# Spreading VectorE's share of the softmax evenly, and running the third query block in halves, in a fused attention and gated-MLP block

## The chip, the cores and the metric

One core of a Trainium2 chip runs the whole program. The metric is the device time of one execution in microseconds; the time before is 909.33 us, the median of three runs (908.4, 909.33 and 910.13).

## The reference, cut to what matters

```python
# S = 2048 rows, D = 640, H = 32 heads of Dh = 20, F = 1728, bf16, one batch
def attention(x, wqkv, wo):
    q, k, v = split_heads(x @ wqkv)                          # each (H, S, Dh)
    p = softmax(einsum("hqd,hkd->hqk", q, k) * Dh ** -0.5)
    return merge_heads(p @ v) @ wo
def glu(x, w_gate, w_up, w_down):
    return ((x @ w_gate) * (x @ w_up)) @ w_down
h  = x + attention(layernorm(x), wqkv, wo)
h2 = h + glu(layernorm(h), w_gate, w_up, w_down)             # the output
```

The two layer norms have no scale and no offset.

## The kernel before

**Units.** The scores of one head for 512 keys-by-queries are the unit of work: a 128x512 tile in PSUM, made of 128 keys and 512 queries, or of two times 128 keys and 256 queries where a pass works on half a query block. There are 2048 such units (32 heads, 16 key tiles, 4 query blocks). Four heads share a group, because a head takes 32 of the 128 partitions (`SLOT`); there are 8 groups (`g` = 0 to 7).

**Segments.** The list `segs` gives the order: for each segment a pass (`PASS`: its query block, first column and width), a group and a range of key tiles. Query block 0 starts in chunks of four key tiles for groups 0 to 3, since keys and values are projected while attention already runs; the rest of block 0, and blocks 1 and 2, go group by group over all 16 key tiles (passes "0", "1", "2": "whole" segments of 64 units). Block 3 goes whole for groups 0 and 1 (`SPLIT_G` = 2, pass "3") and then in halves: pass "A" has its first 256 queries for groups 2 to 7, pass "B" the other 256 ("half" segments of 32 units). Below, A4 is group 4 of pass A.

**Two exponentials.** Most units get their exponential on ScalarE (`nc.scalar.activation`, line 676), three and two units at a time in alternating steps; a step `i` is one such activation, fed by TensorE's score products (line 668). Some units of a segment instead go to VectorE: `on_dve(s)` says how many. Such a unit's scores go to a bank of the ring `mi` (two PSUM banks that all projection and MLP sums use too); VectorE takes them out (line 688, tile `di`), and after every second unit a batch of three integer and bf16 passes follows (lines 571, 573, 576), whose results `dt` and `di` stand for the exponential together. Before the change `on_dve` counts in whole key tiles (four units): 12 of 64 units in a whole segment, and in half segments 8 of 32 for even groups and 4 of 32 for odd ones, none in the chunks; 336 in all. `due` says at which ScalarE unit each VectorE unit is to be issued; `EARLY` and `LEAD` are how far ahead of the segment's start the first is due and how far ahead of its end the last.

**Accumulation.** `emit_AV` multiplies exponentials with values (line 802) into one PSUM bank `acc`. A segment's last product closes it (`close`): VectorE copies the bank to `asb` (line 819), and only then can the next segment's products start. The normalization follows by small DMAs and GpSimd (`norm`), or through TensorE for the segments in `FAST` (`job_norm`).

**Jobs.** All other TensorE work is a queue of jobs, a few products at a time put between the steps by a planner with costs of its own (`fill_step`, `can_work`): projections (`job_proj`, `job_V`), and for each query block a tail (`add_tail`): output projection, layer norm, the gated product (`job_glu`: `u` and `hh`, line 1095) and the last product (`job_y`). A tail is queued once all segments of its rows are normalized: blocks 0, 1 and 2 as a whole with four row tiles, block 3's first half after pass A. The second half of block 3 has a tail of its own behind everything (`last_tail`).

**The head.** The layer norm of the first 512 rows comes first; then steps run while the queue makes four value jobs, and after them the projections of groups 1 to 3. The layer norm of rows 512 to 1023 gets its inverse root by a chain of Newton steps on VectorE (`rstd_steps`), the later ones on GpSimd (`rstd_wait`).

All engines work through their instructions in the order in which the program issues them.

Of the kernel before, what the change touches and what calls it, by code (L numbers as in the profile page):

```python
# [10 lines left out]
BF16 = mybir.dt.bfloat16  # L11
F32 = mybir.dt.float32
I32 = mybir.dt.int32
# [5 lines left out]
P = 128  # L19
# [19 lines left out]
FP = 7  # L39
FPW = 256  # L40
G1 = 4
SPLIT_G = 2
QA = 3 * QB
RES0 = 3
SM_SCALE = float(DH) ** -0.5
# [10 lines left out]
EXP_BIAS = KAPPA - 127.0 * math.log(2.0)  # L56
DB = 2
DW = DB * BANK
LEAD, EARLY = 18, 6
SWITCH = 100  # L60
ROUND = 216
S_NS = SWITCH + ROUND
# [2 lines left out]
EASE, HURRY = -400, -200  # L65
S_LAG = 270
AHEAD = 700
MINJOB = 800
AVLOW = 8
AVMIN = 216  # L70
SLACK = 100
# [5 lines left out]
def kernel(  # L77
# [114 lines left out]
            nc.vector.bn_stats(st[:, h, :], halves[h] if halves else src[:, h * HALF:(h + 1) * HALF])  # L192
        nc.vector.bn_aggr(mv[:, k, :], st[:])

    def rstd_steps(mv, n):
        mb = small.tile([P, n], BF16, name="mb")
        nc.vector.tensor_copy(mb[:], mv[:, :, 0])
        m32 = small.tile([P, n], F32, name="m32")
        nc.vector.tensor_copy(m32[:], mb[:])
        vb = small.tile([P, n], BF16, name="vb", tag="mvb")  # L200
        nc.vector.tensor_copy(vb[:], mv[:, :, 1])
        ve = small.tile([P, n], BF16, name="ve")
        nc.vector.tensor_scalar_add(ve[:], vb[:], EPS_B)
        v = small.tile([P, n], F32, name="v")
        nc.vector.tensor_copy(v[:], ve[:])
        yield
        y = small.tile([P, n], F32, name="y")
        iy = small.tile([P, n], I32, name="iy", tag="mb")
        nc.vector.tensor_scalar(iy[:], v[:].bitcast(I32), 1, None, ALU.arith_shift_right)
        nc.vector.tensor_scalar(y[:].bitcast(I32), iy[:], -1.0, float(0x5F3759DF), ALU.mult, ALU.add)  # L210
        t = small.tile([P, n], F32, name="nt")
        for k in range(3):
            nc.vector.tensor_tensor(t[:], y[:], y[:], ALU.mult)
            nc.vector.scalar_tensor_tensor(t[:], t[:], -0.5, v[:], ALU.mult, ALU.mult)
            nc.vector.scalar_tensor_tensor(y[:], t[:], 1.5, y[:], ALU.add, ALU.mult)
            if k == 0:
                yield
        den = small.tile([P, n], BF16, name="den")
        nc.vector.tensor_tensor(den[:], v[:], y[:], ALU.mult)
        r = small.tile([P, n], F32, name="rstd")  # L220
        nc.vector.reciprocal(r[:], den[:])
        yield (m32, r)

    def rstd_pool(mv, n):
        mvb = small.tile([P, n, 2], BF16, name="mvb", tag="mvb")
        nc.gpsimd.tensor_copy(mvb[:], mv[:])
# [10 lines left out]
    def rstd_wait(mv, n):  # L237
# [2 lines left out]
        while clk["dve"] < until and not forced["on"]:  # L240
            yield WAIT
        yield got

    def rstd_of(mv, n):
        for got in rstd_steps(mv, n):
            pass
        return got

    def ln_apply(dst, src, m32, r, k):
        nc.vector.tensor_scalar(dst, src, m32[:, k:k + 1], r[:, k:k + 1], ALU.subtract, ALU.mult)  # L250
# [120 lines left out]

    PASS = {"0": (0, 0, QB), "1": (1, 0, QB), "2": (2, 0, QB), "3": (3, 0, QB), "A": (3, 0, HW), "B": (3, HW, HW)}
    segs = []
    for ch in range(NB):
        for g in range(G1):
            kind = "copy" if ch == 0 else "last" if ch == NB - 1 else "add"
            segs.append(("0", g, ch * TPB, (ch + 1) * TPB, kind))
    segs += [("0", g, 0, NT, "only") for g in range(G1, NG)]  # L380
    segs += [(p, g, 0, NT, "only") for p in "12" for g in range(NG)]
    segs += [("3", g, 0, NT, "only") for g in range(SPLIT_G)]
    segs += [(p, g, 0, NT, "only") for p in "AB" for g in range(SPLIT_G, NG)]
    FINAL = len(segs) - 1
    FAST = {("2", NG - 1), ("A", NG - 1), ("B", NG - 2)}

    def on_dve(s):
        p, g, lo, hi, kind = segs[s]
        if kind != "only":
            return 0  # L390
        if PASS[p][2] == HW:
            return 2 - g % 2 if s != FINAL else 1
        return 3

    a_units, d_units, due, left = [], [], [], {}
    for s, (p, g, lo, hi, _) in enumerate(segs):
        n = BANK // PASS[p][2]
        groups = list(range(lo, hi, n))
        cut = len(groups) - on_dve(s)
        a0 = len(a_units)  # L400
        a_units += [(s, kt, j) for kt in groups[:cut] for j in range(HPG)]
        own = [(s, kt, j) for kt in groups[cut:] for j in range(HPG)]
        span = len(a_units) - a0
        due += [a0 - EARLY + (span - LEAD + EARLY) * (k + 0.5) / len(own) for k in range(len(own))]
        d_units += own
        left[s] = [n * (cut + 2 * on_dve(s))] * HPG

    LAST_B, LAST_T = NB - 1, [2, 3]
    first_b = [next(k for k, u in enumerate(us) if all(PASS[segs[v[0]][0]][0] == LAST_B for v in us[k:])) for us in (a_units, d_units)]
# [18 lines left out]
    def add(key, gen, front=False):  # L428
        (jobs.appendleft if front else jobs.append)((key, gen, None))
# [471 lines left out]
    def gen_ln(ch):  # L901
        ts = range(ch * TPB, (ch + 1) * TPB)
        while hold(("x", ch)):
            yield WAIT
        mv = small.tile([P, TPB, 2], F32, name="mv")
        for k in range(TPB):
            bn(mv, k, xs[ch][:, k, :])
            yield 930
        for got in (rstd_steps if ch == 1 else rstd_wait)(mv, TPB):
            yield WAIT if got == WAIT else 1100 if ch == 1 else 0  # L910
# [24 lines left out]
    def need_T(key, ch):  # L935
        needs[key] = T_keys(ch)
        return key

    for ch in range(NB):
        if ch:  # L940
            for t in range(ch * TPB, (ch + 1) * TPB):
                add(("T", t), T_of(t))
            if ch + 2 < NB:
                do(("x", ch + 2), lambda ch=ch: more_x(ch + 2))
            add(need_T(("k", 0, ch), ch), job_proj(1, 0, ch))
        for t in range(ch * TPB, (ch + 1) * TPB):
            add(need_T(("v", t, 0), ch), job_V(t, 0))
        for g in range(1, G1):
            if ch == 0:
                add(need_T(("q", 0, g), 0), job_proj(0, g, 0))  # L950
            add(need_T(("k", g, ch), ch), job_proj(1, g, ch))
    for g in range(G1, NG):
        add(need_T(("q", 0, g), 0), job_proj(0, g, 0))
        for ch in range(NB):
# [184 lines left out]
    def add_tail(b, ts):  # L1139
        if b == 0:  # L1140
            do(("open",), open_late)
        key = (b, ts[0])

        def loads():
            if b not in tail_st:
                tail_st[b] = new_st(rows_of(b))
                tail_st[b]["res"] = late["res"]
            load_tail(tail_st[b], ts)
            for fp in range(2):
                load_w(fp, tail_st[b])  # L1150
# [12 lines left out]
        add(("y",) + key, lazy(lambda st: job_y(st, ts)))  # L1163
# [74 lines left out]
    def normed(p, gs):  # L1238
        return all(("n", p, g) in done for g in gs)

    def add_tails():
        if seen["b"] < NB - 1 and normed(str(seen["b"]), range(NG)):
            add_tail(seen["b"], list(range(TPB)))
            seen["b"] += 1
        if not seen["a"] and normed("3", range(SPLIT_G)) and normed("A", range(SPLIT_G, NG)):
            add_tail(LAST_B, [0, 1])
            seen["a"] = True
# [17 lines left out]
    seen = {"b": 0, "a": False, "last": False}  # L1265
    i = 0
    while pos["a"] < len(a_units) or pos["d"] < len(d_units):
        now["i"] = i
# [14 lines left out]
    while acc["next"] < len(segs) or ("loadB",) not in done:  # L1283
        now["i"] = i
        clk["pe"] += 500
        clk["dve"] = max(clk["dve"], clk["pe"])
        act_end[i] = max(clk["pe"], *ring["free"]) + 3000
        work(i)
        emit_AV(i, 2, True)
        dve_fill(act_end[i], True)  # L1290
        run_events(i)
        add_tails()
        i += 1
# [99 lines left out]
```

## Time and profile before

| | |
|---|---|
| median of three runs | 909.33 us |
| the profiled execution's own time | 908.28 us |
| its span in the profile | 906.3 us |
| TensorE busy | 812.8 us (90%) |
| ScalarE busy | 807.9 us (89%) |
| VectorE busy | 712.7 us (79%) |
| GpSimd busy | 182.3 us (20%) |
| first and last exponential on ScalarE start | 17.3 and 846.2 us |
| ScalarE exponentials | 342 of 128x1536 and 343 of 128x1024 |
| VectorE units | 336 |

The profile is of one execution. Its times are microseconds from the span's start; a line of the timeline gives start, length, engine, source line, operation, output and input tile, the number of instructions merged, and in brackets the idle time before them and what ended it. TensorE's busy time is modelled from pipelined products and does not mean that the engine is at its peak.

### The profile page before, as it was taken

To read this page: it belongs to the slowest core of one execution; us is meant where nothing else is said; L and a number is where in the kernel's file an instruction comes from. 1 tells how busy PE (TensorE), PEld (TensorE's weight loads), DVE (VectorE), ACT (ScalarE), POOL (GpSimd) and SP (SyncE) were. 2 spreads that over 40 slices of the span, in tenths; PEclk is the share of its full clock that TensorE was granted. 3 is DMA by queue.
4 is the path that set the end of the run, shared out by engine and by line. 5 is a ranking of instruction groups with operands and counts; after the bars stand their busy time and mean duration, and the time that the engine had idled before them with its cause. 6 is when DMAs were issued, how large, how long until landed. Compare 5 with 4: busy or idle time off the path is not lost. (4 is left out here: it accounts for less than half of the span.)

```text
span 906.3 us, 27993 instructions
## 1 busy us (share of the span) xinstructions
PE 812.8 (90%) x12193; PEld 358.7 (40%) x12205; DVE 712.7 (79%) x1407; ACT 807.9 (89%) x721; POOL 182.3 (20%) x227
## 2 busy tenths in 40 slices
PE   6999999989999899998897988899988988998997
PEld 4343343322334233333243322344433444545775
DVE  7884449898888998987879978978898787789642
ACT  5899999999999999999999999999998888899331
POOL 3110025412213322212214210212041211214000
PEclk8999999999999999999999999999999999999999
DMA  6100001110080322101220121104401000031210
GB/s 197 30 3 1 3 16 27 36 29 14 14 286 16 111 72 73 36 21 30 64 58 3 53 65 45 33 21 114 120 14 44 9 9 22 17 98 51 72 44 18
DMA packets 67856, 45.08 MB, mean 50 GB/s; under 512 B 18504, under 2 KB 63404, under 8 KB 67728
## 3 DMA queue, kind: packets, MB, share of 16 engines
q1 hardware_dynamic: 67728, 43.23, 16.9%
q8 instruction: 97, 1.59, 0.7%
q14 instruction: 31, 0.25, 0.1%
HBM read 35.91 MB, written 7.30 MB: 48 GB/s over the span
## 5 line engine op out<-in xcount | busy, mean ns | idle before, releaser
L676 ACT ACTIVATE E<-sc 128x1536 bf16<-128x1536 f32 (+1 forms) x685 | 790.6, 1253 | 40.4 <-PE mi L668 22.5
L688 DVE TENSOR_SCALAR di<-mi 128x512 int16<-128x512 f32 x336 | 228.2, 683 | 37.8 <-PE mi L668 36.5
L668 PE MATMUL sc<-qa,kT 32*128 32x512 bf16 x1296 | 202.2, 383 | 45.1 <-ACT E L676 39.9
L802 PE MATMUL acc<-E,vx 128*32 128x512 bf16 (+1 forms) x2024 | 228.6, 354 | 6.1 <-DVE asb L819 3.1
L668 PEld LDWEIGHTS <-kT 32*128 32x128 bf16 x2432 | 81.0, 91 | 263.3 <-issue 254.4
L710 POOL TENSOR_TENSOR rr<-rr,powers 128x16 f32<-128x16 f32 (+1 forms) x34 | 90.5, 2661 | 324.4 <-DMA rr<-sums 324.4
L576 DVE TENSOR_TENSOR di<-di,dm 128x1024 bf16<-128x1024 bf16 x168 | 119.2, 709 | 3.9
L802 PEld LDWEIGHTS <-vx 128*32 128x32 bf16 x2840 | 70.3, 95 | 120.0 <-issue 106.7
L668 PE MATMUL mi<-qa,kT 32*128 32x512 bf16 x240 | 92.0, 383 | 0.9 <-DVE di L688 0.8
L293 PE MATMUL mi<-lnT,wp 128*32 128x512 bf16 x1240 | 80.6, 384 | 1.4 <-DVE lnT L265 0.7
L571 DVE TENSOR_SCALAR dm<-di 128x1024 int16<-128x1024 int16 x168 | 77.3, 460 | 2.8
L802 PE MATMUL acc<-dt,vx 128*32 128x512 bf16 (+1 forms) x408 | 74.5, 348 | 0.5 <-DVE dt L573 0.5
L573 DVE TENSOR_SCALAR dt<-di 128x1024 int16<-128x1024 int16 x168 | 74.7, 445 | 0.0
L802 PE MATMUL acc<-di,vx 128*32 128x512 bf16 (+1 forms) x408 | 72.6, 346 | 1.7 <-DVE di L576 1.4
L668 PE MATMUL sc<-qb,kT 32*128 32x256 bf16 (+1 forms) x728 | 65.4, 289 | 8.6 <-ACT E L676 7.7
L293 PE MATMUL mi<-wd,hh 128*32 128x320 bf16 x1391 | 63.9, 304 | 1.4 <-DVE di L688 1.0
L293 PEld LDWEIGHTS <-hh 128*32 128x32 bf16 (+1 forms) x1489 | 46.6, 97 | 21.8 <-issue 8.9
L293 PE MATMUL mi<-ln2T,wu 128*32 128x512 bf16 (+1 forms) x780 | 50.3, 370 | 4.4 <-DVE ln2T L265 1.6
L293 PE MATMUL mi<-ln2T,wg 128*32 128x512 bf16 (+1 forms) x780 | 48.7, 364 | 2.3 <-DVE u L265 1.3
L1095 DVE TENSOR_TENSOR hh<-mi,u 128x512 bf16<-128x512 f32 (+3 forms) x56 | 34.8, 621 | 15.8 <-PE mi L293 14.5
L265 DVE CAST u<-mi 128x512 bf16<-128x512 f32 (+3 forms) x56 | 34.7, 620 | 15.5 <-PE mi L293 15.0
L293 PEld LDWEIGHTS <-wp 128*32 128x32 bf16 x1240 | 31.9, 97 | 32.4 <-issue 10.4
(135 smaller groups left out, 683.1 us busy)
## 6 DMA issues: line engine op xcount, KB each, us to landing
bc<-scr SPq DMA_DIRECT2D x100, 64.0 KB
wu<-in_B_w_up_dram SPq DMA_DIRECT2D x20, 320.0 KB
wg<-in_B_w_gate_dram SPq DMA_DIRECT2D x20, 320.0 KB
qsp<-qa SPq DMA_DIRECT2D x8, 384.0 KB
xr<-in_A_x_dram SPq DMA_DIRECT2D x16, 160.0 KB
out_dram<-xr SPq DMA_DIRECT2D x14, 160.0 KB
wd<-in_B_w_down_dram SPq DMA_DIRECT2D x13, 160.0 KB
xs<-in_A_x_dram SPq DMA_DIRECT2D x3, 640.0 KB
```

What stands on the lines that cost most here:

```text
L265: nc.vector.tensor_copy(dst, src)
L293: nc.tensor.matmul(out[k:k + w, :], lhsT=lhsT[:, k:k + w], rhs=rhs, **flags)
L571: nc.vector.tensor_scalar(m16[:, 0:n], s16, M_MASK, M_BITS, ALU.bitwise_and, ALU.bitwise_or)
L573: nc.vector.tensor_scalar(t16[:, 0:n], s16, E_MASK, E_BITS, ALU.bitwise_and, ALU.bitwise_or)
L576: nc.vector.tensor_tensor(sb[:, 0:n], sb[:, 0:n], mb[:, 0:n], ALU.mult)
L668: nc.tensor.matmul(dst[:, h * w:(h + 1) * w], lhsT=kT[g][SLOT * j:SLOT * (j + 1), (kt + h) * P:(kt + h + 1) * P], rhs=q_of(g, b, c0, w)[SL ...
L676: nc.scalar.activation(e[:, 0:n], sc[:, 0:n], ACT.Exp, bias=EXP_BIAS, scale=SM_SCALE)
L688: nc.vector.tensor_scalar(t[:, k * BANK:(k + 1) * BANK], sd[:], EXP_A, 0.0, ALU.mult, ALU.max)
L710: nc.gpsimd.tensor_tensor(ri, r16, powers[:, 1:2].to_broadcast([P, n]), ALU.pow)
L802: nc.tensor.matmul(acc["t"][SLOT * j:SLOT * (j + 1), 0:w], lhsT=vx[kt][:, VS * h:VS * h + SLOT], rhs=e, start=(j not in acc["new"]), stop= ...
L1095: nc.vector.tensor_tensor(st["hh"][2 * fp + f2][0:M, c0:c0 + n], ps[0:M, 0:n], hold["u"][0:M, 0:n], ALU.mult)
```

## The change

VectorE's units are counted one by one instead of by key tile: 12 of 64 in a whole segment as before, 6 of 32 in every half segment, 4 in the last, and 2 of 16 in each of the four segments of block 0's last chunk. Query block 2 is now run like block 3, groups 0 and 1 whole and the others in halves (passes "E" and "F"), so that its tail falls in two tails of two row tiles. The first layer norm behind the head uses GpSimd like the others. In the queue, value jobs and projections of a chunk take turns. `LEAD` is 14 instead of 18 and `MINJOB` (the room that a job needs to start) 700 instead of 800. In the last loop of the program the accumulation is issued ahead of the jobs.

```diff
-SPLIT_G = 2
+CHUNK_D = (3, 0)
+D_CHUNK, D_WHOLE, D_HALF, D_LAST = 2, 12, 6, 4
+SPLIT_2 = 2
+SPLIT_3 = 2
-LEAD, EARLY = 18, 6
+LEAD, EARLY = 14, 6
-MINJOB = 800
+MINJOB = 700
...
-    PASS = {"0": (0, 0, QB), "1": (1, 0, QB), "2": (2, 0, QB), "3": (3, 0, QB), "A": (3, 0, HW), "B": (3, HW, HW)}
+    PASS = {"0": (0, 0, QB), "1": (1, 0, QB), "2": (2, 0, QB), "3": (3, 0, QB),
+            "E": (2, 0, HW), "F": (2, HW, HW), "A": (3, 0, HW), "B": (3, HW, HW)}
+    SPLIT = {"2": ("EF", SPLIT_2), "3": ("AB", SPLIT_3)}
+    TAILS = [(b, list(range(TPB)), [(str(b), range(NG))]) for b in range(2)]
+    for p, (hs, n) in SPLIT.items():
+        TAILS += [(PASS[p][0], [2 * k, 2 * k + 1], [(p, range(n)), (h, range(n, NG))]) for k, h in enumerate(hs) if h != "B"]
...
-    segs += [(p, g, 0, NT, "only") for p in "12" for g in range(NG)]
-    segs += [("3", g, 0, NT, "only") for g in range(SPLIT_G)]
-    segs += [(p, g, 0, NT, "only") for p in "AB" for g in range(SPLIT_G, NG)]
+    segs += [("1", g, 0, NT, "only") for g in range(NG)]
+    for p, (hs, n) in SPLIT.items():
+        segs += [(p, g, 0, NT, "only") for g in range(n)]
+        segs += [(h, g, 0, NT, "only") for h in hs for g in range(n, NG)]
-    FAST = {("2", NG - 1), ("A", NG - 1), ("B", NG - 2)}
+    FAST = {("F", NG - 1), ("A", NG - 1), ("B", NG - 2)}
     def on_dve(s):
         p, g, lo, hi, kind = segs[s]
         if kind != "only":
-            return 0
+            return D_CHUNK * int((lo // TPB, g) >= CHUNK_D)
         if PASS[p][2] == HW:
-            return 2 - g % 2 if s != FINAL else 1
-        return 3
+            return D_HALF if s != FINAL else D_LAST
+        return D_WHOLE
...
-        groups = list(range(lo, hi, n))
-        cut = len(groups) - on_dve(s)
-        a_units += [(s, kt, j) for kt in groups[:cut] for j in range(HPG)]
-        own = [(s, kt, j) for kt in groups[cut:] for j in range(HPG)]
+        units = [(s, kt, j) for kt in range(lo, hi, n) for j in range(HPG)]
+        cut = len(units) - on_dve(s)
+        a_units += units[:cut]
+        own = units[cut:]
...
-        for got in (rstd_steps if ch == 1 else rstd_wait)(mv, TPB):
+        for got in rstd_wait(mv, TPB):
...
-        for t in range(ch * TPB, (ch + 1) * TPB):
-            add(need_T(("v", t, 0), ch), job_V(t, 0))
+        values = [(("v", t, 0), job_V(t, 0)) for t in range(ch * TPB, (ch + 1) * TPB)]
+        others = []
         for g in range(1, G1):
...
+        while values or others:
+            for some in (values, others):
+                if some:
+                    key, job = some.pop(0)
+                    add(need_T(key, ch), job)
...
-        work(i)
         emit_AV(i, 2, True)
+        work(i)
```

More of the change, by code (lines that the diff above doesn't have):

```diff
@@ L193, in bn @@
         nc.vector.bn_aggr(mv[:, k, :], st[:])
[L195 to L222, printed above, removed]
     def rstd_pool(mv, n):
@@ L242, in rstd_wait @@
         yield got
[L244 to L247, printed above, removed]
     def ln_apply(dst, src, m32, r, k):
@@ L397 @@
         n = BANK // PASS[p][2]
-        groups = list(range(lo, hi, n))
-        cut = len(groups) - on_dve(s)
+        units = [(s, kt, j) for kt in range(lo, hi, n) for j in range(HPG)]
+        cut = len(units) - on_dve(s)
         a0 = len(a_units)
-        a_units += [(s, kt, j) for kt in groups[:cut] for j in range(HPG)]
-        own = [(s, kt, j) for kt in groups[cut:] for j in range(HPG)]
-        span = len(a_units) - a0
-        due += [a0 - EARLY + (span - LEAD + EARLY) * (k + 0.5) / len(own) for k in range(len(own))]
+        a_units += units[:cut]
+        own = units[cut:]
+        due += [a0 - EARLY + (cut - LEAD + EARLY) * (k + 0.5) / len(own) for k in range(len(own))]
         d_units += own
-        left[s] = [n * (cut + 2 * on_dve(s))] * HPG
+        left[s] = [n * (sum(u[2] == j for u in units) + sum(u[2] == j for u in own)) for j in range(HPG)]
     LAST_B, LAST_T = NB - 1, [2, 3]
@@ L908, in gen_ln @@
             yield 930
-        for got in (rstd_steps if ch == 1 else rstd_wait)(mv, TPB):
-            yield WAIT if got == WAIT else 1100 if ch == 1 else 0
+        for got in rstd_wait(mv, TPB):
+            yield WAIT if got == WAIT else 0
         for k, t in enumerate(ts):
@@ L945 @@
             add(need_T(("k", 0, ch), ch), job_proj(1, 0, ch))
[L946 to L947 removed]
+        values = [(("v", t, 0), job_V(t, 0)) for t in range(ch * TPB, (ch + 1) * TPB)]
+        others = []
         for g in range(1, G1):
             if ch == 0:
[L950 to L951 removed]
+                others.append((("q", 0, g), job_proj(0, g, 0)))
+            others.append((("k", g, ch), job_proj(1, g, ch)))
+        while values or others:
[3 more added lines that the diff above has]
+                    add(need_T(key, ch), job)
     for g in range(G1, NG):
@@ L1241, in add_tails @@
     def add_tails():
[L1242 to L1247, printed above, removed]
+        while seen["t"] < len(TAILS):
+            b, ts, sums = TAILS[seen["t"]]
+            if not all(normed(p, gs) for p, gs in sums):
+                return
+            add_tail(b, ts)
+            seen["t"] += 1
     def waiting():
@@ L1263, in idle_products @@
             mm(ROUND)
-    seen = {"b": 0, "a": False, "last": False}
+    seen = {"t": 0, "last": False}
     i = 0
@@ L1287 @@
         act_end[i] = max(clk["pe"], *ring["free"]) + 3000
+        emit_AV(i, 2, True)
         work(i)
-        emit_AV(i, 2, True)
         dve_fill(act_end[i], True)
```

## The prediction

> **What bounds the kernel now.** I read the page's engine rows first, then busy time by stage, then ScalarE's timeline, because the page alone cannot separate ScalarE (89%) from TensorE (90%). The stages cut the run at the first exponential, the end of block 0's chunks, passes 2, A and the last exponential:
>
> ```profile
> core 0: us, PE busy (x) PEld busy (x) DVE busy (x) ACT busy (x) POOL busy (x), PEclk, DMA share, GB/s
> 17.00:139.00 122.00, 113.70 (x1742) 47.62 (x1743) 72.51 (x165) 117.44 (x103) 12.85 (x15) 1.00 0.04 10
> 139.00:435.00 296.00, 270.20 (x3649) 98.71 (x3640) 259.74 (x472) 286.73 (x250) 74.30 (x61) 0.99 0.20 59
> 435.00:682.00 247.00, 221.01 (x3051) 87.25 (x3059) 210.34 (x405) 240.34 (x210) 53.91 (x50) 1.00 0.20 54
> 682.00:847.00 165.00, 148.02 (x3022) 77.51 (x3020) 134.85 (x263) 145.89 (x126) 33.02 (x38) 0.98 0.15 40
> 847.00:906.00 59.00, 50.25 (x676) 39.75 (x668) 23.33 (x66) 10.08 (x25) 0.22 (x1) 0.97 0.13 36
> ```
>
> The reader sees ScalarE idle 4.6, 9.3 and 6.7 us in the first three stages (about 3%), but 165 - 145.89 = 19.1 us in passes A and B. So the exponentials set the pace up to 682; there a second limit appears, and 59 us of TensorE work follow the last exponential. ScalarE's timeline in passes A and B shows where it waits:
>
> ```profile
> 703.69 2.37 ACT L676 ACTIVATE E<-sc 128x1024 bf16<-128x1024 f32 x2 [2.99 <-PE mi L668]
> 707.59 6.88 ACT L676 ACTIVATE E<-sc 128x1024 bf16<-128x1024 f32 x6 [1.53 <-PE sc L668]
> ...
> 733.89 7.24 ACT L676 ACTIVATE E<-sc 128x1024 bf16<-128x1024 f32 x6 [2.00 <-PE mi L668]
> 760.81 4.63 ACT L676 ACTIVATE E<-sc 128x1024 bf16<-128x1024 f32 x4 [2.60 <-PE mi L668]
> 771.31 2.51 ACT L676 ACTIVATE E<-sc 128x1024 bf16<-128x1024 f32 x2 [1.07 <-PE sc L668]
> 775.59 4.75 ACT L676 ACTIVATE E<-sc 128x1024 bf16<-128x1024 f32 x4 [1.77 <-PE mi L668]
> 840.77 6.46 ACT L676 ACTIVATE E<-sc 128x1024 bf16<-128x1024 f32 x6 [1.88 <-PE mi L668]
> ```
>
> Seven brackets hold 13.8 of the 19.1 us. Around the first, all engines' timeline shows the cause:
>
> ```profile
> 700.32 0.40 PE L802 MATMUL acc<-dt,vx 128*32 128x256 bf16 x8
> ...
> 701.16 0.68 DVE L576 TENSOR_TENSOR di<-di,dm 128x1024 bf16<-128x1024 bf16 x1
> 701.90 0.40 PE L802 MATMUL acc<-di,vx 128*32 128x256 bf16 x6 [1.06 <-DVE di L576]
> ...
> 702.39 0.42 DVE L819 COPY asb<-acc 128x256 f32<-128x256 f32 x1 [0.54 <-issue]
> ...
> 702.86 0.40 PE L802 MATMUL acc<-E,vx 128*32 128x256 bf16 x8 [0.57 <-DVE asb L819]
> ```
>
> A2 cannot close before VectorE's last batch (701.84); TensorE waits there 1.06 us, then 0.57 us for the copy, and the score products that ScalarE needs stand behind both. Five brackets (11.0 us) lie at the closes of A2, A4, A6 and B6, all with 8 VectorE units; two (2.8 us) around A7's normalization through TensorE.
>
> **The stall's rule, from the trace.** For each segment I took the time from the start of its last line 688 to the end of the batch that uses it (latency), and from the instruction order the steps between that unit's scores and the close (allowance). A step takes 830 us / 685 = 1.2 us. A2: latency 5.9 us, allowance 3 steps (3.6 us); A4: 5.8 and 4; A6: 5.3 and 3; B6: 3.9 and 3. Those exceed the allowance by 2.3, 1.0, 1.7 and 0.3 us, and cost 4.5, 2.0, 2.6 and 1.9: the excess plus 1.5 us on average. B2 (4.5 us, 5 steps), B4 (4.2, 4) and all but one of the segments with 4 units stay below; A5 (5.3, 4) is over by 0.5 and costs under 0.5. Mean latency is 4.9 us with 8 units, 3.2 with 4, 3.5 over the 22 whole segments.
>
> **The change part by part**, against the profiled 908.28 us (span 906.3 and 2.0 around it), which is 1.05 below the median.
>
> *Fewer units on ScalarE: -2.7.* 342 VectorE units instead of 336. The two forms of the exponential differ by 1467 - 1041 = 426 ns per unit; 6 x 0.426 = 2.6, and two activations fewer save about 0.1 of starting cost. The eight new VectorE units of the last chunk fall where VectorE is busy 10 of 25 us (100 to 125); hidden there, each would otherwise cost some 1.5 us (0.68 + half of 0.46 + 0.45 + 0.71).
>
> *Head: -2.2, between -3.3 and 0.* ScalarE waits 0.79 us at 24.07 and 2.50 at 27.59, the latter for group 1's keys:
>
> ```profile
> 24.07 1.02 ACT L676 ACTIVATE E<-sc 128x1024 bf16<-128x1024 f32 x1 [0.79 <-PE sc L668]
> 27.59 34.38 ACT L676 ACTIVATE E<-sc 128x1536 bf16<-128x1536 f32 x30 [2.50 <-PE sc L668]
> ```
>
> In the new order two value jobs (0.86 us each) stand before them instead of four, and 2.8 us of Newton steps leave VectorE, which had to copy those keys out. The same root took GpSimd 2.9 us at 40.1; GpSimd is free from 17.4. The change adds a wait here: VectorE's first apply (line 256) waits for GpSimd, and value copies and group 2's queries stand behind it. In the order it comes after group 1's keys, so at about 25, and the root is done at about 24 (statistics at 21.2 plus 2.9). The gain is zero if value copies become the next wait.
>
> *Even counts in A and B: -4, between -13.8 and +13.* By the order, allowances of half segments become: E2 to E7 4, 5, 7, 4, 6, 4; F2 to F7 6, 2, 5, 3, 3, 3; A2 to A7 3, 3, 7, 5, 6, 4; B2 to B6 4, 5, 4, 6, 6. So evenness is bought back partly by `LEAD`: six closes have 3 steps or fewer. Latency at 6 units is not in the trace; between 3.2 and 4.9 I take 3.5 to 3.7, the whole segments' (same density, 12 of 64). Then F3 costs 1.2 + 1.5, and the five with 3 steps 0 to 1.6 each, 0.9 on average: 7.2 in all against 11.0; norms by TensorE stay. -4. At 4.9 us: F3 4.0, five at 2.8, six with 4 steps at 1.6: 28; less 11.0, and less some 4 at the closes where the tails are light: +13.
>
> *Block 2 in halves: +1.7, between 0 and +7.* Six closes more. TensorE's 256-wide first products waited 3.1 us for `asb` in 11 closes, 0.28 each: 1.7. The gated sums split in 28 more pieces: the mean run of 20 products takes 1.26 us at 512 and 0.73 at 256, 0.19 more per split, 5.3 us of TensorE; VectorE pays 28 x (2 x 0.423 - 0.688) = 4.4. I cost both at nothing: 90 filler products stand in the new order against 71, so the queue still has holes; without that cover it is +7. The new DMAs on SP (44 more 256-wide broadcasts, 20 fewer of 512, six more weight loads) meet a queue of 16.9% share. The first half tail starts earlier, but the order shows block 3's first tail no earlier: it follows the second half tail. Nothing is credited.
>
> *After the last scores: +0.9.* 380 gated products remain instead of 340, two sums at 0.65 us, less four rounds of accumulation at 0.11. The swap in the last loop moves accumulation ahead of them; `out_most` covers the final normalization already.
>
> Sum: -2.7 - 2.2 - 4 + 1.7 + 0.9 = -6.3: 902.0 on the profiled execution, 903.0 against the median.
>
> [...]
>
> **The rivals.** *All stalls go* (20%): the brackets lie only at 8-unit segments and one norm. -2.7 - 3.3 - 13.8 + 0 + 0.9 = -18.9: 890.4. Against it: the short allowances. *VectorE's batch becomes the wait at most closes* (17%): with 24 half segments instead of 12 and later due units, it decides once latency passes about 4.5 us. For it: VectorE is busy 210 of 247 us in pass 2 and 23.5 of 25 at 675 to 700. -2.7 - 2.2 + 13 + 1.7 + 0.9 = +10.7: 920.0. *TensorE's jobs take over* (11%): then ScalarE's savings buy nothing, since the queue is as long as before: 0 + 1.7 + 0.9 = +2.6, with some of the split's 5.3, 910 to 915; against it: 3% idle on ScalarE until 682. *Products cost issue time* (2%): 80 products of 256 columns run from 849.33 for 2.53 us, 28 ns each, which is columns, four abreast; if a half-wide round took as long as a full one (20 products of 512 columns take 1.26 us, some 0.21 per four), the 500 or so half-wide rounds that the change adds (227 of accumulation, 270 of gated sums) would each cost 0.107 us more, +53 us: 956. [...]
>
> **How the numbers follow.** A measurement of this kernel can tell 0.2% (1.8 us) from no change. Forecast 50% (of it 0.03 within 0.2%), all stalls gone 20%, VectorE 17%, TensorE 11% (half within), issue 2%. Faster 0.47 + 0.20 = 0.67, same 0.03 + 0.05 = 0.08, slower 0.06 + 0.17 + 0.02 = 0.25. The forecast's own range is 896 to 908; 8 in 10 needs most of the fast rival and TensorE's: 891 to 914.
>
> **What would show it.** Right: ScalarE idle under 17 us in the last 165 us before its last exponential, no bracket at 24 to 28 of over 1 us, idle in pass 2 up by under 4. Wrong: brackets of 2 us at E and F closes with line 576 ending late, or the last exponential no earlier than 846.

## The result, and the profile after

The changed kernel is slower: 914.65 us against 909.33 (medians of 13 runs each). The ratio over all runs is 1.0068 with a 95% interval of 1.0046 to 1.0090, or +6.2 us (the means differ by 6.2, the medians by 5.3). The prediction's range was 891 to 914. The profiled execution took 913.35 us, 5.1 more than the one of before. First the engine row and the granted clock in 40 slices on the page of the changed kernel, then, in the page of the kernel before, the same clock row:

```profile
PE 828.4 (91%) x13596; PEld 386.5 (42%) x13609; DVE 718.4 (79%) x1438; ACT 807.9 (89%) x719; POOL 191.9 (21%) x250
PEclk8999999999979999999999999999799999997999
```

```profile
PEclk8999999999999999999999999999999999999999
```

No engine's share has changed by more than a point, but for the weight loads (PEld, 40 to 42%); three slices now show a clock of 0.7. Busy time by stage of the changed kernel, in the columns of the prediction's table, tells the stages apart:

```profile
139.00:435.00 296.00, 273.32 (x3654) 98.67 (x3655) 258.32 (x469) 281.95 (x244) 74.25 (x60) 0.97 0.21 59
435.00:682.00 247.00, 223.66 (x3979) 105.34 (x3986) 204.66 (x401) 231.38 (x201) 56.62 (x63) 0.97 0.22 55
682.00:847.00 165.00, 152.63 (x3353) 84.89 (x3349) 139.34 (x294) 155.81 (x135) 36.46 (x43) 0.97 0.18 46
```

ScalarE's idle time falls from 19.1 to 165 - 155.81 = 9.2 us in passes A and B, where the change aimed. It rises from 6.7 to 15.6 us in the stage before it and from 9.3 to 14.1 in the one before that. ScalarE's timeline of the changed kernel (start, length, in brackets the wait and its releaser) has these among its waits:

```profile
26.28 1.45 ACT L650 ACTIVATE E<-sc 128x1536 bf16<-128x1536 f32 x1 [1.42 <-PE sc L642]
31.80 11.53 ACT L650 ACTIVATE E<-sc 128x1024 bf16<-128x1024 f32 x10 [1.04 <-PE sc L642]
497.61 3.40 ACT L650 ACTIVATE E<-sc 128x1024 bf16<-128x1024 f32 x3 [1.55 <-PE mi L642]
659.20 2.37 ACT L650 ACTIVATE E<-sc 128x1024 bf16<-128x1024 f32 x2 [4.28 <-PE sc L642]
776.57 5.79 ACT L650 ACTIVATE E<-sc 128x1024 bf16<-128x1024 f32 x5 [1.21 <-PE mi L642]
831.30 2.37 ACT L650 ACTIVATE E<-sc 128x1024 bf16<-128x1024 f32 x2 [1.30 <-PE mi L642]
```

The largest, 4.28 us at 659.20, is new and no close of a segment. (Line 650 is the prediction's 676, line 642 its 668.) To compare kernels stage by stage I use one number, ScalarE's *loss*: the time from one exponential's start to the next, less such a time where nothing delays it (1.348 us behind a 1536-wide one, 0.904 behind a 1024-wide one; the very shortest in the trace are 1.330 and 0.904), summed. It is added up from the trace of one execution of each kernel:

| loss, us | 17-139 | 139-340 | 340-435 | 435-635 | 635-695 | 695-770 | 770-end | sum |
|---|---|---|---|---|---|---|---|---|
| before | 6.0 | 10.5 | 5.1 | 9.1 | 4.5 | 14.8 | 8.6 | 58.7 |
| after | 7.1 | 18.1 | 4.1 | 11.9 | 10.7 | 4.1 | 9.7 | 65.7 |
| e1: even counts alone | 6.0 | 10.4 | 4.4 | 11.5 | 4.5 | 8.0 | 4.8 | 49.5 |
| e8: even counts, new head | 6.1 | 10.2 | 3.7 | 10.1 | 4.9 | 8.3 | 5.2 | 48.5 |
| e7: even counts, both constants | 6.1 | 18.3 | 5.0 | 9.4 | 4.1 | 10.4 | 7.0 | 60.4 |
| e16: before, both constants | 6.6 | 19.0 | 5.7 | 7.9 | 6.1 | 12.1 | 7.1 | 64.4 |
| e2: after, block 2 whole | 7.1 | 17.7 | 4.1 | 12.3 | 4.3 | 8.4 | 7.0 | 61.0 |
| e9: after, root ahead | 8.6 | 13.5 | 4.3 | 11.7 | 5.5 | 4.9 | 8.3 | 56.7 |

From first to last exponential the kernel before takes 828.9 us and the changed one 833.6: the undelayed times alone sum to 770.2 and 767.9, and the loss is 58.7 and 65.7. What follows the last exponential's start is 60.2 and 60.1 us. So 10.7 us of loss went out of 695 to 770 as intended, and 7.6 came in at 139 to 340 and 6.2 at 635 to 695. The experiments ask what brought these two.

One execution is a rough measure. Up to 498 us the changed kernel, e2, e3, e9 and e12 issue the same work in the same order on ScalarE, VectorE and GpSimd, yet lose 18.1, 17.7, 16.4, 13.5 and 15.8 us at 139 to 340. With the old constants and block 2 whole the loss there is 10.2 to 10.6 (before, e1, e8, e15; 14.7 in e6, with its filler), so these groups stay apart, but a difference of under 5 us between two rows tells little.

### The profile page after: what moved, and what is told of

Read it like the earlier page. It is cut to its first block, busy times and chain, and to the rows that moved or that the text cites. A ratio compares the mean times of both kernels' runs of the same rounds, so it can differ in the third digit from the quotient of the medians.

```text
span 911.2 us, 30947 instructions
## 1 busy us (share of the span) xinstructions
PE 828.4 (91%) x13596; PEld 386.5 (42%) x13609; DVE 718.4 (79%) x1438; ACT 807.9 (89%) x719; POOL 191.9 (21%) x250
## 3 DMA queue, kind: packets, MB, share of 16 engines
q1 hardware_dynamic: 74592, 45.34, 18.3%
## 4 chain that ended last, share of the span: by engine, by line
PE 44%; ACT 33%; DVE 14%; issue 5%; DMA 2%; POOL 0%; SPq 0%; ACTq 0%; DVEq 0%
ACT E L650 33%; PE mi L262 18%; PE sc L642 11%; PE acc L776 9%; DVE di L662 4%; PE f L262 3%; DVE di L550 2%; DVE dm L545 1%; DVE dt L547 1%; DVE st L195 1%; PE mi L642 1%; DMA scr<-rr 1%; PE mi L1240 1%; DVE qa L241 1%; DVE hh L1074 1%
## 5 line engine op out<-in xcount | busy, mean ns | idle before, releaser
L650 ACT ACTIVATE E<-sc 128x1536 bf16<-128x1536 f32 (+2 forms) x683 | 790.6, 1248 | 44.8 <-PE sc L642 21.0
L776 PE MATMUL acc<-E,vx 128*32 128x256 bf16 (+1 forms) x2332 | 232.7, 335 | 5.5 <-DVE asb L793 2.8
L642 PE MATMUL sc<-qa,kT 32*128 32x512 bf16 (+1 forms) x1600 | 204.7, 344 | 35.5 <-ACT E L650 27.9
L776 PEld LDWEIGHTS <-vx 128*32 128x32 bf16 x3300 | 77.4, 96 | 122.5 <-issue 111.2
L550 DVE TENSOR_TENSOR di<-di,dm 128x1024 bf16<-128x1024 bf16 x171 | 124.8, 730 | 3.5
L642 PE MATMUL mi<-qa,kT 32*128 32x512 bf16 (+1 forms) x320 | 96.3, 337 | 1.7 <-DVE qa L241 0.7
L776 PE MATMUL acc<-dt,vx 128*32 128x256 bf16 (+1 forms) x484 | 77.9, 331 | 0.4 <-DVE dt L547 0.3
L776 PE MATMUL acc<-di,vx 128*32 128x256 bf16 (+1 forms) x484 | 75.8, 329 | 0.8 <-DVE di L550 0.8
L1074 DVE TENSOR_TENSOR hh<-mi,u 128x256 bf16<-128x256 f32 (+1 forms) x70 | 37.0, 528 | 18.3 <-PE mi L262 17.2
L234 DVE CAST u<-mi 128x256 bf16<-128x256 f32 (+1 forms) x70 | 37.0, 528 | 12.5 <-PE mi L262 11.7
```

The source lines that it names most:

```text
L234: nc.vector.tensor_copy(dst, src)
L550: nc.vector.tensor_tensor(sb[:, 0:n], sb[:, 0:n], mb[:, 0:n], ALU.mult)
L642: nc.tensor.matmul(dst[:, h * w:(h + 1) * w], lhsT=kT[g][SLOT * j:SLOT * (j + 1), (kt + h) * P:(kt + h + 1) * P], rhs=q_of(g, b, c0, w)[SL ...
L650: nc.scalar.activation(e[:, 0:n], sc[:, 0:n], ACT.Exp, bias=EXP_BIAS, scale=SM_SCALE)
L776: nc.tensor.matmul(acc["t"][SLOT * j:SLOT * (j + 1), 0:w], lhsT=vx[kt][:, VS * h:VS * h + SLOT], rhs=e, start=(j not in acc["new"]), stop= ...
L1074: nc.vector.tensor_tensor(st["hh"][2 * fp + f2][0:M, c0:c0 + n], ps[0:M, 0:n], hold["u"][0:M, 0:n], ALU.mult)
```

## The experiments

Ratios are to the kernel before, run on the same chip at the same time, with their 95% interval; "us" of a ratio is its distance from 1 times 909.33. A difference between two such ratios is uncertain by about 0.3%, 3 us. The indented text under an experiment is what was expected before it ran. Three theories were open after the result: that the halves of block 2 cost time, that the constants `LEAD` and `MINJOB` do, or that the lower clock does by itself.

**e1: even counts alone.** The kernel before, with the new counting but the old rest:

```diff
+D_CHUNK, D_WHOLE, D_HALF, D_LAST = 0, 12, 6, 4
-            return 2 - g % 2 if s != FINAL else 1
-        return 3
+            return D_HALF if s != FINAL else D_LAST
+        return D_WHOLE
```

> Before, with one part of the change alone: 6 VectorE units in each half segment of block 3 instead of 8 and 4 in turn (4 in the last); all else as before. Theory C (clock): ScalarE's time is lost where TensorE's granted clock is halved, and that follows a stretch in which TensorE stood idle for about 2 of 3.4 us; even counts take away the idle stretches at the closes of A2 and A6, so the two half-clock stretches near 704 and 772 us go and passes A and B lose about 10 us less: 897 to 902 us. Theory H (short allowances): even counts with LEAD 18 help less, 904 to 909 us. Under both the granted clock before 690 us stays as in the kernel before.

900.66 us, 0.9927 [0.9905, 0.9948]: -6.6 us, with two VectorE units fewer than before (334). The even counts are a gain; the loss at 695 to 770 falls from 14.8 to 8.0 and behind it from 8.6 to 4.8. The time lies in the range of Theory C, but not by its cause: the half-clock time of a whole execution, worked out from the mean granted clock, is 22.5 us against 21.8 before (medians).

**e2: the changed kernel with block 2 whole.**

```diff
-    SPLIT = {"2": ("EF", SPLIT_2), "3": ("AB", SPLIT_3)}
+    SPLIT = {"3": ("AB", SPLIT_3)}
-    FAST = {("F", NG - 1), ("A", NG - 1), ("B", NG - 2)}
+    FAST = {("2", NG - 1), ("A", NG - 1), ("B", NG - 2)}
```

> The changed kernel with block 2 whole again and one tail of four row tiles. Theory C: the half-clock stretches at 643 and 657 us come from block 2's second half tail (TensorE waits for the layer norm's root) and go with it; those at 257 and 309 us come from the queue's hole before tail 0 and stay: 907 to 911 us, last exponential 4 to 6 us earlier than in the changed kernel. Theory H (halves themselves cost TensorE and VectorE time): the time falls by 8 us or more, to under 907, and the loss outside the half-clock stretches (49 us before and after) falls by 5 or more too.

906.5, 0.9988 [0.9963, 1.0013]. Halving block 2 is worth 1.0068 - 0.9988 = 0.8%, +7.3 us. The loss at 635 to 695 is back at 4.3; that at 139 to 340 stays at 17.7, so the halves did not bring it.

**e3: whole segments, but block 2's tail in two.** `SPLIT_2 = 8` in the changed kernel, with segment 7 of pass 2 in `FAST`.

> The changed kernel with block 2 in whole segments, but its tail still in two tails of two row tiles, both queued at the end of the pass. Tells half segments from half tails. Theory C: a half tail has no second pair of row tiles whose products cover the layer norm's root, so there is at least one stretch of 3 us with TensorE idle before a tail's transposes and a half clock after it, as in the changed kernel: 911 to 917 us. Theory H: half segments are the cost, so the time is that of block 2 whole, within 2 us.

912.8, 1.0048 [1.0024, 1.0072]. The last exponential starts at 842.4, well before the 851.1 of the changed kernel, but 540 gated products are left behind the last scores (380 in the changed kernel), and what follows takes 68.5 us. The split moved the work to the end, so this one does not price the tails. But its trace shows that two half tails need not stall TensorE: the first statistics are ready at 664.0, the root starts at 664.1, and TensorE waits for none of the normalized rows (no wait for VectorE of over 0.8 us at 600 to 700).

**e4: the kernel before without its idle products.** The call of `idle_products` is taken out.

> Before without its filler products (idle_products is not called; they add zeros or write a bank that nobody reads). Theory C: TensorE's idle windows at the holes of the queue near 210, 300, 440 to 500 and 640 us pass 2 us, the clock is halved in several more of them, and each 3.4 us at half clock costs 1 to 1.5 us of ScalarE time: with 5 to 10 more such stretches the time is 915 to 925 us. Without theory C: no change, or faster by up to 2 us, since 59 products less stand in TensorE's queue.

923.7, 1.0186 [1.0156, 1.0216]. The half-clock time between the first and the last exponential rises from 10.2 to 37.5 us, but this exponential starts only 3.0 us later (849.2); the other 11 us lie behind it (71.5 instead of 60.2), since the planner's order changed too. It does not price the clock.

**e5: the changed kernel with its idle steps filled.** Products of a zero weight tile are added to `acc` in the steps where TensorE idles, 128 rounds; all other instructions keep their order.

```diff
+        for _ in range(QB // w):
+            for j in range(HPG):
+                nc.tensor.matmul(acc["t"][SLOT * j:SLOT * (j + 1), 0:w], lhsT=zeros[:], rhs=kT[0][:, 0:w], start=False, stop=False)
```

> The changed kernel, every instruction in its place, and 128 rounds of filler more (four products of a zero weight, 32 columns of the array each, added to the open accumulation bank), in steps where the profile of the changed kernel has TensorE idle for over 1.5 of some 3.4 us. Theory C: with the holes filled the half-clock stretches at 257, 309 and 497 us go; those after the 3.5 us wait for the layer norm's root (643 to 664) and perhaps that at 824 stay. The median half-clock time falls from 53 to 25 to 40 us, and at 0.2 to 0.3 us of time for each us of it the time is 907 to 911 us. Theory H (the halves cost TensorE time): 27 us more of TensorE work in a full queue, so 915 to 925 us.

915.63, 1.0077 [1.0052, 1.0101]. The clock row of its page is full but for one slice:

```profile
PEclk9999999999999999999999999999899999999999
```

The half-clock time fell from 53 to 26 us (medians of its runs), and the time did not. Either the clock costs little or the filler costs what it gives; the hole at 652 to 659 stayed, since there TensorE waits for the half tail's rows (6.46 us for `ln`), and in this execution it was longer (8.12 us of ScalarE's time, a loss of 14.0 at 635 to 695).

**e6: the same filler on e1.**

> Before with even counts (the first experiment's kernel) and 127 rounds of the same filler in its own idle steps. Theory C: half-clock time falls from 22 us to under 12 and the time by 1 to 4 us, to 897 to 900 us. Without it: 901 to 906 us, since the filler stands in TensorE's queue.

905.4, 0.9949 [0.9928, 0.9970], 2.0 us slower than e1 by the ratios, which is within their uncertainty, though the half-clock time fell from 22.5 to 10.8 us (medians). The filler takes TensorE time itself (TensorE is busy 838.7 us on e5's page, 828.4 on the changed kernel's), so e5 and e6 do not price the clock; but less half clock alone made neither kernel faster.

**e7: both constants on e1.**

```diff
-LEAD, EARLY = 18, 6
+LEAD, EARLY = 14, 6
-MINJOB = 800
+MINJOB = 700
```

> Before with even counts, and LEAD 14 and MINJOB 700 as in the changed kernel. By the allowance rule VectorE's last units come about 4 ScalarE units later, so more closes wait: 902 to 908 us against 900.7 for even counts alone. If the later units cost nothing: 899 to 902, and what block 2 whole (906.5) lost against even counts alone is the head's or the chunk's.

909.47, 1.0002 [0.9984, 1.0019]: +6.8 us on e1, and the loss at 139 to 340 goes from 10.4 to 18.3. Of TensorE's waits between 140 and 850 us, the one for the copy out of `acc` at the closes grows, here in e7 and then in e1 (total, times, longest; their lines 805 and 822 are the prediction's 802 and 819):

```profile
PE acc L805 <- DVE asb L822: 6.2, 5, 2.5
```

```profile
PE acc L805 <- DVE asb L822: 1.5, 3, 0.7
```

4.5 of the 6.2 us stand in two closes between 139 and 340, which run whole segments of 12 units in every version. In the changed kernel this wait is only 2.8 us in all, so the trace shows the constants' cost at such closes for e7, and not for the changed kernel.

**e8: the new head on e1.** `rstd_wait` for the first layer norm, and value jobs and projections in turns.

> Before with even counts and the head's part of the change (value jobs and projections in turn, first root on GpSimd). As forecast the head gains 2.2 us: 898 to 899. The changed kernel's profile shows 5.0 us lost in the first chunk against 3.8 before, so the other reading is a loss of 1 to 2 us there, and projections that end sooner leave a longer hole before tail 0 with a half clock in it: 901 to 905 us.

898.66, 0.9884 [0.9860, 0.9907]: 3.9 us better than e1 by the ratios, and the fastest kernel of this study, 10.5 us below the kernel before.

**e9: in the changed kernel, the half tail's root ahead of one scaling.** Only GpSimd's order changes, at one place (the timelines below show what stands there).

```diff
-            later(4, lambda: scale(bc))
+            later(10 if (p, g) == ("F", 6) else 4, lambda: scale(bc))
```

> The changed kernel with one move on GpSimd alone: the scaling of segment F6, which waits 10 us for a broadcast that stands behind eight weight loads, is issued behind the five small operations of a half tail's layer norm root instead of ahead of them; TensorE's and VectorE's orders stay. Theory Q (a queue): the 3.5 us in which TensorE waits for that root, ScalarE's 4.3 us wait and the half clock at 657 us go, so 4 to 6 us less: 908 to 911 us. Theory H (half-wide work is the cost of the halves): the wait moves elsewhere, 913 to 916 us.

908.66, 0.9991 [0.9971, 1.0010]: -7.0 us. All engines' timeline of the changed kernel shows what it removed:

```profile
644.20 0.98 SPq L1045 DMA_DIRECT2D qa<-in_B_w_gate_dram  x1
645.28 1.00 SPq L686 DMA_DIRECT2D scr<-rr  x1
649.86 1.72 SPq L689 DMA_DIRECT2D bc<-scr  x4
653.32 0.73 POOL L693 TENSOR_TENSOR on<-asb,bc 128x256 bf16<-128x256 f32 x1 [10.14 <-DMA bc<-scr]
654.17 0.19 POOL L200 CAST mvb<-mv 128x4 bf16<-128x4 f32 x1
655.68 0.70 POOL L208 TENSOR_TENSOR rstd<-den,powers 128x2 f32<-128x2 bf16 x1
656.41 0.80 DVE L219 TENSOR_SCALAR ln<-xr,m,rstd 128x640 bf16<-128x640 bf16 x2 [4.48 <-POOL rstd L208]
656.92 0.69 PE L299 MATMUL mi<-ident,ln 128*128 128x128 bf16 x5 [3.48 <-DVE ln L219]
```

Read it downwards. Eight weight loads of 240 or 320 KB each (line 1045, issued from 637.75 to 645.2) stand ahead of F6's normalization (lines 686 and 689) on the queue of SP, the engine that issues these DMAs. F6's inverse sums are ready at 641.35, their store is issued 3.9 us later and lands some 4.6 us after that, and the scaling starts 12.0 us after the sums, where e2 has 4.9 to 7.0 at 500 to 640. So GpSimd waits 10.14 us for the broadcast `bc`, and the root of the first half tail, five small instructions, stands behind that scaling: its statistics are ready at 645.32, and it starts at 654.17. VectorE then waits 4.48 us for the root, TensorE 3.48 for the normalized rows, and ScalarE 4.28 for the scores behind them. The long wait alone does no harm: five other normalizations between 500 and 640 take 9.3 to 14.2 us, with no wait of ScalarE of over 0.8 us there. It cost ScalarE 4.28 us here, where a small instruction that TensorE needs stands behind it. In e9 the root comes out before the broadcast:

```profile
642.49 0.19 POOL L200 CAST mvb<-mv 128x4 bf16<-128x4 f32 x1 [2.13 <-DVE mv L196]
644.02 1.17 POOL L208 TENSOR_TENSOR rstd<-den,powers 128x2 f32<-128x2 bf16 x1
650.70 1.31 POOL L693 TENSOR_TENSOR on<-asb,bc 128x256 bf16<-128x256 f32 x1 [5.52 <-DMA bc<-scr]
```

and no wait of ScalarE between 636 and 658 is over 1.2 us. (Its loss at 139 to 340 is lower too, 13.5, where the edit changes nothing; the ratio, not the sum of that row, is the price.)

**e10 and e11: one constant each on e1.** `LEAD = 14`, and `MINJOB = 700`.

> Before with even counts and LEAD 14 alone (MINJOB stays 800); LEAD 14 and MINJOB 700 together gave 909.5 us against 900.7. Theory L (VectorE's last units come too late for the closes of whole segments): 906 to 911 us. Theory M (the smaller room for a job lets jobs delay score products): 900 to 903 us.

> Before with even counts and MINJOB 700 alone (LEAD stays 18). Theory L: 900 to 903 us. Theory M: 906 to 911 us.

919.72, 1.0098 [1.0066, 1.0130], and 911.18, 1.0023 [1.0000, 1.0045]: +15.5 and +8.7 us on e1, and +6.8 together (e7). Each reorders the whole queue; the prices do not add.

**e12: half segments in block 2, but one tail.**

> The changed kernel with block 2 in half segments, but one tail of four row tiles for it. Theory Q: the root's wait belongs to the half tail that meets the weight loads, so it goes, and the time is that of block 2 whole plus 40 gated products at the end (1 to 2 us): 907 to 910 us. Theory H: half segments themselves cost 6 us or more: 912 to 917 us.

913.26, 1.0045 [1.0018, 1.0071], 5.2 us above e2, in the range of Theory H. Its profiled execution (909.45, loss 61.3) is the fastest of its ten runs and hardly differs from e2's, so the trace does not say where the 5.2 us lie. Nor do the prices add: 7.0 for the root's wait (e9) and 5.2 for half segments without half tails are more than the 7.3 of both.

**e13: the changed kernel with the old constants; e14: e13 with e9's edit.**

> The changed kernel with LEAD 18 and MINJOB 800 as before. If the constants cost the changed kernel what they cost on even counts (8.8 us): 904 to 908 us, with the loss at 139 to 340 us (18 us in the changed kernel) down to 10 or 11. By its instruction order 520 gated products are left after the last scores instead of 380, seven sums at some 0.65 us, so 4 us of it may come back at the end: 908 to 911 us. If the constants are neutral there: 914 to 919 us.

> The same with the layer norm's root ahead of F6's scaling on GpSimd, as in the ninth experiment. If the queue's loss is independent of the constants: 6 us less than the kernel without it in this call. If the wait at that place came from the changed kernel's own timing: within 2 us of it.

920.59, 1.0140 [1.0108, 1.0171], and 920.8, 1.0146 [1.0115, 1.0176]. Against what e7 suggested, the old constants make the changed kernel slower. The loss at 139 to 340 is 24.2 us in e13's profiled execution, the slowest of its six, and 19.3 in e14's. Both have one wait that holds most of the excess (8.48 us on ScalarE in e14); in e13:

```profile
281.91 0.49 DVE L1002 TENSOR_TENSOR xr<-mi,xr 128x320 bf16<-128x320 f32 x1 [7.32 <-DMA xr<-in_A_x_dram]
285.10 1.45 ACT L650 ACTIVATE E<-sc 128x1536 bf16<-128x1536 f32 x1 [8.47 <-PE mi L642]
```

The rows `xr` of the first tail are loaded on SP behind 16 stores of spilled queries (`qsp`, 267.7 to 278). And e9's edit brings nothing here. GpSimd waits even longer for F6's broadcast in e13:

```profile
669.34 0.73 POOL L693 TENSOR_TENSOR on<-asb,bc 128x256 bf16<-128x256 f32 x1 [17.28 <-DMA bc<-scr]
```

but the half tail's statistics are ready only at 670.23, so the root loses nothing by standing behind it. The cost of that order belonged to the changed kernel's own timing.

**e15: the swapped last loop on e8.**

> Even counts, the new head and the new last loop with the old constants and block 2 whole: 897 to 900 us, since the last loop alone moves accumulation ahead of jobs where the final norm is already covered. It is the version of the changed parts that should beat both kernels; over 903 us would mean that the eighth experiment was a lucky order.

900.85, 0.9930 [0.9905, 0.9955], 4.2 us above e8 by the ratios, with 3 us of uncertainty: accumulation ahead of the jobs is no gain.

**e16: both constants on the kernel before.**

> Before with LEAD 14 and MINJOB 700 alone, counts 8 and 4 as before. If VectorE's later units cost at the closes of whole segments (139 to 635 us), as in the seventh experiment: 914 to 920 us, with 5 us or more of the loss there. If the constants only shift where holes and stalls fall: within 4 us of the kernel before, on either side.

913.26, 1.0065 [1.0033, 1.0097]: +5.9 us, with the loss at 139 to 340 up by 8.4. It is the same stage as in e7 and in the changed kernel.

**e17: e13 with the spills behind the first tail's jobs; e18: the same move on e8.**

```diff
-    for g in range(NG):
-        do(("spill", g), lambda g=g: spill(g))
...
+        if b == 0:
+            for g in range(NG):
+                do(("spill", g), lambda g=g: spill(g))
```

> The changed kernel with LEAD 18 and MINJOB 800, and the sixteen spill transfers of the queries issued after tail 0's jobs instead of ahead of its loads; the orders of TensorE, VectorE and ScalarE stay. Theory Q: the wait of 7.3 us for tail 0's input rows, ScalarE's 8.5 us and the half clock at 277 go: 8 to 12 us less than the same kernel without it (920.6), 909 to 913 us. Theory K (the constants' effect on order is the cost): within 3 us of 920.6.

> Even counts and the new head (898.7 us) with the spill transfers later. Theory Q: its trace has no wait of over 1 us at tail 0's loads, so within 2 us of 898.7, and at best 1 to 2 us less where the clock no longer halves near 209. It would be the fastest version if the hole before tail 0 narrows.

e17: 910.51, 1.0040 [1.0019, 1.0061], 9.1 us below e13. No wait of ScalarE of over 0.6 us is left between 257 and 314, and the exponentials run on where e13 stood still:

```profile
273.20 14.03 ACT L650 ACTIVATE E<-sc 128x1024 bf16<-128x1024 f32 x12 [0.17 <-PE sc L642]
```

So the order on SP's queue caused that wait. e18: 907.26, 0.9988 [0.9969, 1.0007], 9.5 us above e8, against the forecast: the stores now stand ahead of the second tail's rows, as its timeline shows.

```profile
468.68 0.49 DVE L1000 TENSOR_TENSOR xr<-mi,xr 128x320 bf16<-128x320 f32 x1 [5.99 <-DMA xr<-in_A_x_dram]
470.94 1.45 ACT L650 ACTIVATE E<-sc 128x1536 bf16<-128x1536 f32 x1 [5.49 <-PE sc L642]
```

**What the change is made of,** by these ratios: even counts -6.6 (e1), head -3.9 (e8), both constants +6.8 (e7), block 2 in halves +7.3 (after against e2), and +2.6 left for the chunk's units and the last loop, by difference. The sum is +6.2 by construction; the parts do interact (e13), so it tells what each did in this order, not what each is worth anywhere.

## Why the prediction was wrong

It forecast 903.0 us, 6.3 less than before; the ratio says 6.2 more. Two steps failed: the constants `LEAD` and `MINJOB` had no term, and block 2 in halves was priced too low, since its new DMAs were weighed by a mean share. The other terms follow in the prediction's order.

**Fewer units on ScalarE (-2.7): about right.** One exponential of 128x1536 and two of 128x1024 fewer, with one of 128x512 more at the end, lower the sum of undelayed times by 2.3 us. No run has the last chunk's eight units by themselves, so that they stay hidden on VectorE is not shown, nor is the 0.1 us of starting cost by itself, which was an estimate.

**Even counts (-4): right in sign.** For block 3 alone they gave -6.6 us with the old constants (e1 against before) and -5.7 with the new ones (e7 against e16), each with some 3 us of uncertainty. ScalarE's idle time in the last 165 us before the last exponential is 165 - 155.82 = 9.2 us, well under the 17 named. Where seven brackets of 1.07 to 2.99 us stood in passes A and B, the changed kernel has two, of 1.21 and 1.30. But the stall's rule set one mean latency against each allowance, and the two go together: in the changed kernel the six closes with 3 steps or fewer (A2, A3, F3, F5, F6, F7) had latencies of 2.2 to 3.1 us, and the long ones (A4 6.8, B5 5.9, B6 7.2, E4 6.4, F2 5.9) had 6 or 7 steps. The mean over 23 segments was 4.1, above the 3.5 to 3.7 taken, and yet the stalls priced at 7.2 us, F3's 2.7 among them, did not come. One bracket was also misread: that at 707.59 lies in a stretch of half clock (704.1 to 707.5), so some of what was put to VectorE may have been the clock.

**`LEAD` and `MINJOB`: no term.** The prediction let them in only through the allowances of half segments. They cost +6.8 (e7) and +5.9 us (e16), at 139 to 340, where all segments are whole and no count changes. This is the first step that failed: a constant of the planner acts on every segment, and it was costed where the eye was. In e7 closes that wait for VectorE show there; in the changed kernel as much loss is spread over waits of 1.5 us and less, with 13.65 us of half clock from 257.6, and no run prices the constants there alone. Why each alone costs more than both is open, and so is what the best pair would be for the changed kernel: 18 and 800 make it 6.5 us slower by another wait (e13), and with that removed it is at 910.51 (e17).

**Block 2 in halves (+1.7): +7.3.** The second step that failed. The closes themselves were costed well enough: TensorE's 256-wide first products wait 2.8 us for `asb` in the whole of the changed kernel, less than before (3.1). The mistake that the runs show is the sentence that the new DMAs on SP "meet a queue of 16.9% share". A share is an average; at 645 the queue held eight weight loads, and GpSimd's small root stood behind the broadcast that waited for them. And "the first half tail starts earlier", credited with nothing, was a cost in this order: its transposes came due while the root stood there, and TensorE had nothing else to do for 3.48 us. Half tails alone do not bring this (e3, e13). e9 takes back 7.0 us by moving one scaling in GpSimd's order, with 3 us of uncertainty. What stays open is e12, where half segments without half tails cost about 5 us.

**Head (-2.2): the size agrees, the place does not.** e8 gives -3.9, with 3 us of uncertainty. But the sign named for it, no bracket of over 1 us at 24 to 28, failed: 1.42 us stands at 26.28 and 1.04 at 31.80, and the loss up to 139 does not fall (6.0 in e1, 6.1 in e8, 7.1 after). The waits moved inside the head; where the gain lies is not shown, so the agreement in size may be luck.

**After the last scores (+0.9): 0.** What follows the last exponential's start stays at 60 us. The last loop's swap, which the prediction gave no cost, is among the suspects for the +2.6 that is left: on e8 it cost 4.2 us, with 3 us of uncertainty (e15).

**The rivals.** *VectorE's batch becomes the wait* did not come: no 2 us bracket stands at an E or F close with line 576 (550 after) late, although idle time in pass 2's stage rose by 9.0 us instead of under 4. The prediction's other sign of being wrong did come: the last exponential starts at 851.1, later than 846. *TensorE's jobs take over* named 910 to 915, where the time fell, but by chance and not by its cause: e9 issues the same products in the same order and is 7.0 us faster, and e1 turns ScalarE's savings into time. *All stalls go* was near for 695 to 770 (4.1 us of loss left) and wrong elsewhere. *Products cost issue time* (956) is far off.

**The clock,** which the prediction did not weigh. Between the first and the last exponential TensorE's granted clock is half (0.50 in the trace, else 1.00) in stretches of 3.41 us or multiples of it, 10.2 us of them in the profile of before and 44.4 in that after. By the profile's busy times, which are modelled, TensorE is idle for 1.0 to 3.4 of the 3.41 us ahead of each stretch (1.2, 1.6 and 1.4 before; 1.9, 1.0, 2.4, 1.2, 3.4 and 1.3 after). Theory C's "about 2 of 3.4 us" is near their mean in the changed kernel (1.9); how much idle time brings a half clock, the traces do not fix. ScalarE's loss that falls in these stretches and the 3.41 us ahead of them is 9.4 us before and 17.0 after, as much as the growth from 58.7 to 65.7. That does not make the clock the cause, for the waits lie in the same places: e1 has the half-clock time of the kernel before (22.5 and 21.8 us of a whole execution) and is 6.6 us faster, and e5 has half that of the changed kernel (26 and 53) and is not. What the low clock costs by itself stays open.

## What to carry to other kernels

Price a DMA by what stands on its queue at that moment, and a small instruction by what the engine ahead of it is waiting for: a mean share hides both, and in this kernel three such places were worth 7 to 10 us each (e9, e17, e18). Such a wait cost nothing where nothing that is needed stood behind it (e13's 17.28 us: 920.59 us with that order, 920.8 without it in e14). A constant that a planner uses everywhere needs a term for every stage, and its effect does not carry over to a neighbouring version. When a change bundles several edits, time each against the same base: the two good ones here, even counts and the new head, make a kernel of 898.66 us, 1.2% faster than before.

## What the runs showed of the hardware that was not expected

Between executions of one kernel, the time goes with the clock, but with a small slope: over 294 runs of all versions, each compared with its own kernel's mean, 1 us more of half-clock time (worked out from the mean granted clock) goes with 0.21 us more time (correlation 0.62). That is no price for the clock: in e5 products of zeros took the half-clock time from 53 to 26 us, which at 0.21 would give 5.5 us, and the time stayed where it was. Whether these products cost as much, or ScalarE's wait behind the half tail, 8.12 us in e5's trace instead of 4.28, took it back, is not shown.
